# Converting V and the first-MLP weights in smaller pieces, each behind a softmax: an attention-and-MLP kernel on one core

## The chip, the cores and the metric

The kernel runs on one core of one Trainium2 chip. The metric is device time in microseconds (us) of one execution, less is better. Three runs of the kernel before gave 1021.73, 1009.07 and 1010.79 us; their median is 1010.79 us.

## The reference, cut to what matters

Attention over 4 batches, 8 heads, 576 positions and head size 64, with a position bias made by a small network, and then two MLPs over the 2304 tokens of width 512. All arrays are 32 bit floats.

```python
scores = scale * q @ k.T + bias        # bias[h] = relu(x @ w1 + b1) @ w2, x = log1p|i-j| / log1p(max(i,1))
attn = exp(scores - max(scores)); attn = attn / (sum(attn) + 1e-09)
x = attn @ v                           # heads side by side: 2304 x 512
h = max(max(x @ moe_w1, x @ moe_w2), x @ moe_w3)   # 512 -> 768
x = h @ moe_w_out                      # 768 -> 512
h = x @ moe2_w_in                      # 512 -> 2048
g = where(h >= 1, h, where(h <= -1, 0, (h + 1)**2 / 4))
out = g @ moe2_w_out                   # 2048 -> 512
```

In the first MLP `h` is just the largest of the three products. To keep 32 bit accuracy with 16 bit matmuls, an operand is split into a high and a low 16 bit part with a power-of-two scale, and three products of parts are added.

## The kernel before, in words

**Slots.** The queries are cut into five row blocks (four of 128 rows, one of 64). One head of one batch of one row block is a *slot*; there are 144. Slots 0 to 31 are row block 0 (batch b is slots 8b to 8b+7), slots 32 to 63 are row block 1, and so on. The loop at line 903 goes over the slots. For slot i it traces loads ahead (`prefetch`), the score matmuls of the next slot (`emit_s`, L691), the softmax of the slot (`emit_soft`: DVE adds the bias and takes the row extreme, L705; ACT takes the exponent, L707; the probabilities are split into 16 bit parts by ACT L723 and POOL L724 and L725, and a transposing DMA on SP turns them, L727), and the probability-times-V matmuls of slot i-3 (`emit_pv`, L747). In row block 0, odd slots of batches 0 and 1 are turned by TensorE instead (L712 to L719). "The softmax of slot 32" means its L705.

**Work that rides along.** In row block 0 other work is hung on chosen slots:

- `conv_moe(ft)`, one call for each of six columns `ft` of the first MLP's weights (w1, w2, w3). The weights arrive as 64 bit words; `decode` (L462 to L465) makes 32 bit numbers of them, `sum_scale` (L481, L483) finds a scale with TensorE and DVE, and three calls of `split` make the 16 bit parts: ACT writes the high part (L157), DVE the low part (L158), of 128x512 elements each. The slots are in `PRM["cm"]`: 0, 3, 6, 9, 13, 16. Raw weights lie in borrowed places. Column 4's are loaded after column 0's splits, and column 5's (L450) after column 3's splits, into the same bytes. Columns 3 and 5 lie in the buffer of the bias of row block 1.
- V: `v_load(b)` loads batch b (L325, L327), `v_max(b)` finds its scale (L335 and what follows), `v_split(b)` makes two halves (`c` = 0, 1) of 128x1280 elements with the same `split` (L157, L158), clears a strip (POOL, L606) and stores each half to DRAM for the later row blocks (SP, L607, 640 KB each, eight in all). Raw V of batches 1 to 3 shares one place, so the load of batch b+1 waits for the splits of batch b.
- The bias of row block 1: 18 groups (`bias_group`, L389 to L405), traced from slot 16 on and only once all six columns are converted. The softmax of slot 32 needs all 18.

**What sets the order.** The framework gives each instruction a priority by the place where it was traced, simulates the engines with durations of its own, and puts on each engine's queue, of what is ready by that simulation, what was traced first. `sooner("bias")` moves the bias groups 400 places ahead. `tc.issue_after(x)` adds one rule: what is traced inside it and runs on x's engine comes behind x in that engine's queue. `behind(i)` does that with the last L705 for slots below 4. On the chip each queue then runs in that order. `next_mlp` (L784) hands out the first-MLP matmuls (`mlp1`, L802) as long as their column is converted.

Of the kernel before, what the change touches and what calls it, by code (L numbers as in the profile page):

```python
# [20 lines left out]
def kernel(ctx: ExitStack, tc: tile.TileContext, qt, kt, vr, small, mw1, mw2, mw3, mwo, win, wo2, out):  # L21
# [8 lines left out]
    P = 128  # L30
# [15 lines left out]
        vm=[0, 0, 8, 15],  # L46
        vs=[0, 0, 11, 19],
        wo=38,
        cm=[0, 3, 6, 9, 13, 16],
        veng='vv',  # L50
        weng='vvv',
        peng='vv',
# [40 lines left out]
    def st(shape, dt, tag):  # L93
        return sb.tile(shape, dt, tag=tag, name=tag, bufs=BUFS.get(tag, 1))
# [59 lines left out]
    def split(hi, lo, src, scale, eng):  # L154

        if eng == "v":
            A.activation(hi, src, AF.Copy, scale=scale)  # L157
            V.scalar_tensor_tensor(lo, src, scale, hi, ALU.mult, ALU.subtract)  # L158
        else:
            G.tensor_tensor(src, src, (scale.unsqueeze(2) if len(src.shape) == 3 else scale).to_broadcast(src.shape), ALU.mult)  # L160
            A.activation(hi, src, AF.Copy)
            G.tensor_tensor(lo, src, hi, ALU.subtract)

    if True:
# [307 lines left out]
        def by_k(t):  # L472
            return t.rearrange("p (k f) -> p k f", k=KK)
# [12 lines left out]
        def conv_moe(ft):  # L486

            zs, ys = [], []
            for i in range(3):
                ys.append(wm[:, ft, i].rearrange("p s k c -> p (s k c)").bitcast(U32))  # L490
                zs.append(decode(moe_raw[3 * ft + i], None, ys[-1]))
            s = c_sn[:, ft:ft + 1]
            sum_scale(s, ys)
            for i in range(3):
                split(wm[:, ft, i, 0], wm[:, ft, i, 1], by_k(zs[i]), s, WENG[i])
            if ft == 0:
                moe_load(4)
            if ft == 3:
                moe_load(5)

        def conv_wo():

# [90 lines left out]
            wo_done.append(1)  # L593


        def v_split(b):

            if b % 2:
                w = wo.bitcast(F16).rearrange("p f d -> p (f d)")[:, 0:5120].rearrange("p (x s c) -> p x s c", x=2, s=10)
                vv = [w[:, 0], w[:, 1]]  # L600
            else:
                vv = [st([P, 10, 256], F16, "v") for _ in range(2)]
            for c in range(2):
                t = vv[c]
                split(t[:, 0:5], t[:, 5:10], vf(b)[:, :, 256 * c:256 * c + 256], c_sv[:, b:b + 1], VENG[c])
                G.memset(t[64:128, 9], 0.0)  # L606
                SP.dma_start(v_d[b, c], t)  # L607
                kbox[("v", 0, b, c)] = t

        c_s1, c_rb = newcol(), newcol(B)  # L610

# [81 lines left out]
        def halves(t):  # L693
            return t.rearrange("p (a c) -> p a c", a=2)

        last_soft = [None]

        def emit_soft(i):
            u, s = slots[i]
            if s == 0:  # L700
                u.sums = st([P, H], F32, "sums")
            h = s if u.j == SJ else HEADS[s]
            sn = st([P, S], F32, "sp")
            mx = st([P, 1], F32, "mx")
            last_pair[0] = V.tensor_tensor_reduce(halves(sn), sbox.pop(i)[:, :, :288], halves(bias_sb[u.j][:, h]), -0.125, 3e38, ALU.add, ALU.min, mx)  # L705
            pf = sn
            last_soft[0] = A.activation(pf, sn, AF.Exp, scale=-1.0, bias=mx, accum_out=u.sums[:, h:h + 1])  # L707
            if u.j == 0 and u.b < 2 and s % 2:

                pa, pe = mlp_ps(), mlp_ps()[0:64, :P]  # L710
                for c in range(4):
                    T.transpose(pa[:, P * c:P * c + P], pf[:, P * c:P * c + P], ident)  # L712
                T.transpose(pe, pf[:, 512:], ident)
                pt = st([P, 9, P], F16, "pt")
                pa = pa.rearrange("p (c i) -> p c i", c=4)
                A.activation(pt[:, 0:4], pa, AF.Copy)
                A.activation(pt[0:64, 4], pe, AF.Copy)
                V.tensor_tensor(pt[:, 5:9], pa, pt[:, 0:4], ALU.subtract)
                V.tensor_tensor(pt[64:128, 4], pe, pt[0:64, 4], ALU.subtract)  # L719
                ptbox[i] = pt  # L720
                return
            hl = st([P, 2 * S], F16, "phl")
            A.activation(hl[:, :S], pf, AF.Copy)  # L723
            G.tensor_tensor(hl[:, S:S + 64], pf[:, 512:], hl[:, 512:S], ALU.subtract)  # L724
            G.tensor_tensor(hl[:, S + 64:], pf[:, :512], hl[:, :512], ALU.subtract)  # L725
            pt = st([P, 9, P], F16, "pt")
            SP.dma_start_transpose(out=pt, in_=hl)  # L727
            ptbox[i] = pt

        PVSEQ = [(c, c) for c in range(5)] + [(c, 5 + c) for c in range(5)] + [(5 + c, c) for c in range(4)]  # L730
# [53 lines left out]
        def next_mlp(ready):  # L784

            if not mlp_q:
                return None
            if ready:
                return mlp_q.pop(0)
            for x, (f, a) in enumerate(mlp_q):  # L790
                if f is mlp1:
                    return mlp_q.pop(x) if order_of(a[0]) < 2 and a[1] < NF1 - len(conv_left) else None

        def mlp1(key, ft, i, c=slice(0, 256)):

# [94 lines left out]
        for gq in range(0, 18, 2):  # L890
            with tc.issue_after(coef_lo.ins):
                bias_pair(gq)
            while conv_left and PRM["cm"][6 - len(conv_left)] <= gq - 18:
                conv_moe(conv_left.pop(0))
        first_mask.append(last_pair[0])
        emit_s(0)
        with behind(0):
# [20 lines left out]
            return xts[j]  # L918

        early = {}  # L920
        for f, at, *a in [(v_max, "vm", 1), (v_split, "vs", 1), (v_load, "vl", 2), (v_max, "vm", 2), (v_split, "vs", 2), (v_load, "vl", 3), (v_max, "vm", 3), (v_split, "vs", 3)]:
            early.setdefault(PRM[at][a[0]], []).append((f, *a))
        early.setdefault(PRM["vm"][3], []).append((v_scales,))

        def queue_mlp(key, c):
            mlp_q.extend((mlp1, (key, ft, w, c)) for ft in range(NF1) for w in range(3))
# [3 lines left out]
        for i in range(NS + LAG + 1):  # L930
# [20 lines left out]
            if i < NS:  # L951
                with sooner("v"):
                    if PRM["ef"]:
                        for f, *a in early.get(i, ()):
                            with behind(i), tc.issue_after(last_score[0].ins) if f is v_max else nullcontext():
                                f(*a)
                with sooner("w"):
                    while conv_left and PRM["cm"][6 - len(conv_left)] <= i:
                        with behind(i):
                            conv_moe(conv_left.pop(0))  # L960
                b_at, b_n = PRM["bias"][min(u.j, 2)]
                with sooner("bias"):
                    for _ in range(rate("bias", (27 if u.j == 2 else 18) / b_n) if at >= b_at and not conv_left else 0):
                        if bias_q:
                            a = bias_q.pop(0)
                            a = (*a, new_xt(a[0]))
                            if a[0] == SJ:
                                bias_short(*a)
                            else:
                                bias_group(*a, B1[cnt["b"] % len(B1)])  # L970
                                cnt["b"] += 1
# [292 lines left out]
```

## Time and profile before

| | us |
|---|---|
| median of 3 runs (lowest, highest) | 1010.79 (1009.07, 1021.73) |
| profiled execution | 1012.1 |
| its span, first to last instruction | 1010.3 |
| PE busy in the span | 927.0 |
| DVE, ACT, POOL busy in the span | 700.4, 600.4, 511.7 |

Mean granted TensorE clock 0.964 of full speed. Busy time says how much of the span an engine had an instruction in hand, also when that instruction ran at the lower clock. In a row of the trace the square bracket is how long the engine stood idle before the instruction and what released it; "x3" means that three like instructions are merged in one row, and the duration is then that of the three together.

### The profile page before, as it was taken

The numbers are of one execution on the slowest core, as the hardware profiler recorded it, in microseconds if no ns is written. First come the engines' busy times: TensorE is split into PE (matmuls) and PEld (weight loads), VectorE is DVE, ScalarE is ACT, GpSimd is POOL, SyncE is SP. The second block draws the span as 40 slices with busy tenths as digits, with TensorE's granted clock in tenths as the row PEclk, the third lists the DMA queues.
The fourth block names the chain that finished last, engine by engine and source line by source line (L and its number), as shares of the span: only waits on it lengthen the run. The fifth ranks groups of instructions, "written<-read, shape, count | busy, mean of one in ns | idle before, by whom it ended". The sixth has DMA issues, their size and how long they took to land. (4 is left out here: it accounts for less than half of the span.)

```text
span 1010.3 us, 25953 instructions
## 1 busy us (share of the span) xinstructions
PE 927.0 (92%) x10258; PEld 757.4 (75%) x10258; DVE 700.4 (69%) x1551; ACT 600.4 (59%) x1194; POOL 511.7 (51%) x734
## 2 busy tenths in 40 slices
PE   5758889889999999999999888998999999999996
PEld 5636668678888878778777777543588888888885
DVE  8987877767756686556455487886686587586565
ACT  4788865855656545868577689543354444444342
POOL 4132577666777765646457011997134343344442
PEclk8777979999999999999999999999999999999999
DMA  9896989998998979999999654010020010000000
GB/s 301 247 290 140 245 190 229 207 237 170 207 259 186 187 180 209 215 223 235 209 188 197 184 196 137 22 35 8 1 85 22 1 43 23 1 22 13 10 22 22
DMA packets 238970, 141.47 MB, mean 140 GB/s; under 512 B 187520, under 2 KB 217728, under 8 KB 238336
## 3 DMA queue, kind: packets, MB, share of 16 engines
q1 hardware_dynamic: 238688, 139.55, 58.6%
q8 instruction: 80, 1.31, 0.5%
q14 instruction: 42, 0.34, 0.1%
q10 hardware_dynamic: 160, 0.26, 0.1%
HBM read 79.68 MB, written 15.27 MB: 94 GB/s over the span
## 5 line engine op out<-in xcount | busy, mean ns | idle before, releaser
L802 PEld LDWEIGHTS <-aw 128*128 128x128 f16 x2160 | 190.3, 99 | 46.2 <-issue 24.6
L802 PE MATMUL pm<-xT,aw 128*128 128x256 f16 (+1 forms) x1812 | 202.3, 264 | 7.4 <-ACT hl L829 2.6
L725 POOL TENSOR_TENSOR phl<-sp,phl 128x512 f16<-128x512 f32 x136 | 161.3, 1186 | 0.0
L707 ACT ACTIVATE sp<-sp,mx 128x576 f32<-128x576 f32 x144 | 110.4, 767 | 68.0 <-DVE mx L705 67.7
L691 PE MATMUL s<-k,qz 64*128 64x288 f32 (+1 forms) x576 | 126.2, 449 | 15.4 <-DVE mx L705 13.0
L724 POOL TENSOR_TENSOR phl<-sp,phl 128x64 f16<-128x64 f32 x136 | 49.8, 366 | 178.7 <-ACT phl L723 153.2
L705 DVE CUSTOM_DVE_ANT_0 sp<-s,ab 128x576 f32<-128x576 f32 x128 | 93.3, 752 | 28.4 <-POOL phl L725 10.4
L1142 ACT ACTIVATE sp<-pm,vec 128x256 f32<-128x256 f32 x112 | 61.4, 556 | 81.3 <-PE pm L1125 78.2
L691 PEld LDWEIGHTS s<-k,qz 64*128 64x128 f32 (+1 forms) x576 | 69.1, 195 | 34.6 <-DVE mx L705 15.3
L723 ACT ACTIVATE phl<-sp 128x576 f16<-128x576 f32 x136 | 89.8, 672 | 4.7 <-DMA pt<-phl 3.8
L747 PEld LDWEIGHTS <-pt 128*128 128x128 f16 x1792 | 73.0, 100 | 25.2 <-DMA pt<-phl 16.2
L1146 POOL TENSOR_TENSOR hh<-hh 128x128 f32<-128x128 f32 x56 | 32.9, 588 | 106.4 <-DVE hh L1144 90.3
L747 PE MATMUL pav<-v,pt 128*128 128x64 f16 x1568 | 70.5, 196 | 12.3 <-DMA pt<-phl 11.9
L1125 PEld LDWEIGHTS <-ab 128*128 128x128 f16 x756 | 73.8, 98 | 9.2
L1143 DVE SCALAR_TENSOR_TENSOR hh<-pm,vec,sp 128x256 f32<-128x256 f32 x112 | 52.5, 478 | 33.5 <-ACT sp L1142 33.2
L824 PE MATMUL pm<-hh,wo 128*128 128x256 f16 x558 | 71.3, 279 | 2.6 <-POOL hh L814 1.0
L824 PEld LDWEIGHTS <-wo 128*128 128x128 f16 x648 | 62.2, 100 | 14.7 <-issue 6.5
L814 POOL TENSOR_TENSOR hh<-hm,hh 128x256 f16<-128x256 f32 (+1 forms) x60 | 44.8, 746 | 51.9 <-ACT hh L813 51.7
L1164 PEld LDWEIGHTS <-xT 128*128 128x128 f16 x588 | 57.4, 98 | 7.8 <-ACT xT L1151 1.2
L1164 PEld LDWEIGHTS <-wo 128*128 128x128 f16 x588 | 57.5, 98 | 6.7
L809 DVE SCALAR_TENSOR_TENSOR hm<-pm,hm 128x256 f32<-128x256 f32 (+1 forms) x108 | 42.0, 389 | 28.6 <-PE pm L802 12.3
L1147 POOL TENSOR_TENSOR hh<-hh 128x128 f32<-128x128 f32 x56 | 26.2, 468 | 68.6 <-DVE hh L1144 66.3
(300 smaller groups left out, 1999.0 us busy)
## 6 DMA issues: line engine op xcount, KB each, us to landing
k<-in_k_dram SPq DMA_DIRECT2D x64, 288.0 KB, 3.8
v<-v_d SPq DMA_DIRECT2D x24, 640.0 KB, 4.9
ws<-in_moe_w_out_dram SPq DMA_DIRECT2D x15, 512.0 KB, 4.9
ws<-in_moe_w_in_dram SPq DMA_DIRECT2D x9, 512.0 KB, 6.0
x_d<-hl SPq DMA_DIRECT2D x36, 128.0 KB, 2.5
qz<-in_q_dram SPq DMA_DIRECT2D x16, 256.0 KB, 4.5
ab<-in_moe_w_dram SPq DMA_DIRECT2D x8, 512.0 KB, 9.8
qz<-x_d SPq DMA_DIRECT2D x4, 1024.0 KB, 4.8
```

Of the source, the lines that this page charges most:

```text
L691: last_score[0] = T.matmul(sbox[i + r][:, c, :288], q[p, s if u.j == SJ else s // 2], k[p, 288 * c:288 * c + 288], start=True, stop=True)
L705: last_pair[0] = V.tensor_tensor_reduce(halves(sn), sbox.pop(i)[:, :, :288], halves(bias_sb[u.j][:, h]), -0.125, 3e38, ALU.add, ALU.min, mx)
L707: last_soft[0] = A.activation(pf, sn, AF.Exp, scale=-1.0, bias=mx, accum_out=u.sums[:, h:h + 1])
L723: A.activation(hl[:, :S], pf, AF.Copy)
L725: G.tensor_tensor(hl[:, S + 64:], pf[:, :512], hl[:, :512], ALU.subtract)
L747: T.matmul(u.pav[:, 64 * h:64 * h + 64], pt[:, c], v[:, sl, 64 * (h % 4):64 * (h % 4) + 64], **kw)
L802: T.matmul(o, wm[:, ft, i, wp, kk], x_rhs(key, xp, kk) if n == 256 else x_rhs(key, xp, kk)[:, c], start=(x == 0), stop=(x == 11))
L824: T.matmul(pm, wo16[:, ft, wp, P * d:P * d + P], hh[:, ft, hp], start=(ft == 0 and y == 0), stop=(ft == NF1 - 1 and y == 2))
L1125: T.matmul(pm, w[:, wp, kk], x2t[ORDER[y]][:, kk, xp, 256 * sub:256 * sub + 256], start=(x == 0), stop=(x == 11))
L1142: A.activation(r, pm, AF.Relu, scale=c_ch[:, f], bias=c_half)
L1143: V.scalar_tensor_tensor(t, pm, c_c[:, f], r, ALU.mult, ALU.max)
L1164: T.matmul(m[x], gl[:, gp, i], w[:, wp], start=(start and z == 0 and x % 2 == 0), stop=(stop and z == 2 and (x % 2 == 1 or x == 6)))
```

## The change: what it does, and the diff

- `conv_moe` becomes a generator: decode, scale and the first of the three splits come at the column's slot, the second split one slot later, the third one after that. The second and third are traced inside `issue_after` the last L705 and the last L707. The slots of columns 4 and 5 become 12 and 14 (from 13 and 16). The loads that follow columns 0 and 3 come after the third split. The bias groups and `mlp1` ask for finished columns (`conv_done`), where before they asked for started ones.
- `v_split` takes one half at a time, inside the same two `issue_after`. V of batch 1: halves at slots 0 and 8 (both at 0 before). Batch 2: load at slot 8 (2), scale at 12 (8), halves at 13 and 15 (11). Batch 3: load at 15 (11), scale at 19 (15), halves at 20 and 22 (19).
- The stores of V: batch 0 stays with its split; batches 1, 2, 3 are stored at slots 11, 27 and 30, inside `issue_after` the last transposing DMA. Before, each store followed its split.

```diff
-        cm=[0, 3, 6, 9, 13, 16],
+        cm=[0, 3, 6, 9, 12, 14],
...
             for i in range(3):
+                if i:
+                    yield
                 split(wm[:, ft, i, 0], wm[:, ft, i, 1], by_k(zs[i]), s, WENG[i])
             if ft == 0:
                 moe_load(4)
             if ft == 3:
                 moe_load(5)
+            conv_done.append(ft)
+
+        conv_done, conv_open = [], []
...
-        def v_split(b):
+        def v_split(b, cs=(0, 1)):
...
-                vv = [st([P, 10, 256], F16, "v") for _ in range(2)]
-            for c in range(2):
+                vv = {c: st([P, 10, 256], F16, "v") for c in cs}
+            for c in cs:
                 t = vv[c]
                 split(t[:, 0:5], t[:, 5:10], vf(b)[:, :, 256 * c:256 * c + 256], c_sv[:, b:b + 1], VENG[c])
                 G.memset(t[64:128, 9], 0.0)
-                SP.dma_start(v_d[b, c], t)
                 kbox[("v", 0, b, c)] = t
+                if b == 0:
+                    v_store(b, c)
+
+        def v_store(b, *cs):
+
+            for c in cs or (0, 1):
+                SP.dma_start(v_d[b, c], kbox[("v", 0, b, c)])
...
-        last_soft = [None]
+        last_soft, last_turn = [None], [None]
...
-            SP.dma_start_transpose(out=pt, in_=hl)
+            last_turn[0] = SP.dma_start_transpose(out=pt, in_=hl)
...
-                    return mlp_q.pop(x) if order_of(a[0]) < 2 and a[1] < NF1 - len(conv_left) else None
+                    return mlp_q.pop(x) if order_of(a[0]) < 2 and a[1] < len(conv_done) else None
...
-            while conv_left and PRM["cm"][6 - len(conv_left)] <= gq - 18:
-                conv_moe(conv_left.pop(0))
...
-        for f, at, *a in [(v_max, "vm", 1), (v_split, "vs", 1), (v_load, "vl", 2), (v_max, "vm", 2), (v_split, "vs", 2), (v_load, "vl", 3), (v_max, "vm", 3), (v_split, "vs", 3)]:
-            early.setdefault(PRM[at][a[0]], []).append((f, *a))
-        early.setdefault(PRM["vm"][3], []).append((v_scales,))
+        for i, f, *a in [(0, v_max, 1), (0, v_split, 1, (0,)), (8, v_split, 1, (1,)), (8, v_load, 2), (11, v_store, 1), (12, v_max, 2), (13, v_split, 2, (0,)), (15, v_split, 2, (1,)), (15, v_load, 3),
+                         (19, v_max, 3), (19, v_scales), (20, v_split, 3, (0,)), (22, v_split, 3, (1,)), (27, v_store, 2), (30, v_store, 3)]:
+            early.setdefault(i, []).append((f, *a))
...
-                            with behind(i), tc.issue_after(last_score[0].ins) if f is v_max else nullcontext():
-                                f(*a)
+                            with behind(i), tc.issue_after(last_score[0].ins) if f is v_max else tc.issue_after(last_turn[0].ins) if f is v_store else nullcontext():
+                                if f is v_split:
+                                    with tc.issue_after(last_pair[0].ins), tc.issue_after(last_soft[0].ins):
+                                        f(*a)
+                                else:
+                                    f(*a)
                 with sooner("w"):
+                    for g in list(conv_open):
+                        with tc.issue_after(last_pair[0].ins), tc.issue_after(last_soft[0].ins):
+                            if next(g, g) is g:
+                                conv_open.remove(g)
                     while conv_left and PRM["cm"][6 - len(conv_left)] <= i:
                         with behind(i):
-                            conv_moe(conv_left.pop(0))
+                            conv_open.append(conv_moe(conv_left.pop(0)))
+                            next(conv_open[-1])
...
-                    for _ in range(rate("bias", (27 if u.j == 2 else 18) / b_n) if at >= b_at and not conv_left else 0):
+                    for _ in range(rate("bias", (27 if u.j == 2 else 18) / b_n) if at >= b_at and len(conv_done) == NF1 else 0):
```

## Rows read from the trace of the kernel before

**Rows 1.** Windows by stage: us, busy us (count) of each engine, granted clock, DMA share, GB/s.

```profile
31.00:148.00 117.00, 87.95 (x896) 66.53 (x893) 97.24 (x217) 94.80 (x185) 48.36 (x61) 0.80 0.90 216
148.00:175.00 27.00, 24.55 (x549) 23.02 (x547) 22.20 (x44) 13.14 (x35) 22.06 (x27) 1.00 0.95 236
175.00:231.00 56.00, 47.52 (x582) 38.64 (x580) 37.67 (x111) 38.17 (x86) 31.66 (x43) 0.97 1.01 210
231.00:400.00 169.00, 167.10 (x2378) 141.96 (x2376) 117.39 (x279) 100.38 (x244) 117.97 (x155) 1.00 0.94 202
```

**Rows 2.** Timeline of ACT: start us, us, operation; exponents of slots 0 and 31.

```profile
36.79 0.76 ACT L707 ACTIVATE sp<-sp,mx 128x576 f32<-128x576 f32 x1
...
147.89 0.78 ACT L707 ACTIVATE sp<-sp,mx 128x576 f32<-128x576 f32 x1 [0.59 <-DVE mx L705]
```

**Rows 3.** Timeline of DVE and ACT: end of column 5, first bias write, softmax of slot 32.

```profile
134.57 0.79 DVE L158 SCALAR_TENSOR_TENSOR aw<-ab,vec,aw 128x512 f16<-128x512 f32 x1
135.39 0.47 ACT L403 ACTIVATE ab<-pm,vec 128x256 f32<-128x256 f32 x1 [1.26 <-DVE aw L158]
...
174.27 0.76 DVE L705 CUSTOM_DVE_ANT_0 sp<-s,ab 128x576 f32<-128x576 f32 x1 [0.82 <-POOL ab L405]
```

**Rows 4.** Timeline of DVE and PE around 60 us: batch 1's second half, softmax, scores.

```profile
58.10 1.54 DVE L158 SCALAR_TENSOR_TENSOR wo<-ws,vec,wo 128x1280 f16<-128x1280 f32 x1
...
62.56 0.74 DVE L705 CUSTOM_DVE_ANT_0 sp<-s,ab 128x576 f32<-128x576 f32 x1
63.37 2.29 PE L691 MATMUL s<-k,qz 64*128 64x288 f32 x4 [5.41 <-DVE mx L705]
```

**Rows 5.** Timeline of SP, PE and DVE, 61 to 80 us, and one window.

```profile
61.85 1.11 SPq L607 DMA_DIRECT2D v_d<-wo  x1
...
65.82 5.62 SPq L727 DMA_TRANSPOSE pt<-phl  x1
...
77.08 0.93 PE L747 MATMUL pav<-v,pt 128*128 128x64 f16 x14 [3.80 <-DMA pt<-phl]
...
79.54 0.76 DVE L705 CUSTOM_DVE_ANT_0 sp<-s,ab 128x576 f32<-128x576 f32 x1 [4.97 <-PE pm L713]
...
63.00:77.00 14.00, 7.85 (x54) 5.05 (x54) 9.92 (x23) 12.62 (x25) 2.36 (x3) 0.62 1.19 303
```

**Rows 6.** Timeline of ACT, DVE and SP: batch 2's halves, columns 3 and 5.

```profile
94.45 2.60 ACT L157 ACTIVATE v<-ws,vec 128x1280 f16<-128x1280 f32 x2
94.90 0.15 DVE L141 TENSOR_SCALAR vec<-tcol 128x1 uint32<-128x1 uint32 x1
98.77 2.04 ACT L157 ACTIVATE aw<-ab,vec 128x512 f16<-128x512 f32 x3
...
102.09 1.10 SPq L450 DMA_DIRECT2D ab<-in_moe_w_dram  x2
...
111.82 0.68 ACT L462 ACTIVATE ab<-ab 128x512 f32<-128x512 f32 x1 [2.08 <-DMA ab<-in_moe_w_dram]
```

**Rows 7.** Timeline of ACT: batch 3's halves, last decode step of column 5.

```profile
118.85 2.60 ACT L157 ACTIVATE wo<-ws,vec 128x1280 f16<-128x1280 f32 x2
...
122.13 0.65 ACT L465 ACTIVATE aw<-ab 128x512 bf16<-128x512 f32 x1
```

**Rows 8.** Line L158, weight splits on DVE: count, ns min/median/max, first and last start.

```profile
L158 DVE SCALAR_TENSOR_TENSOR aw<-ab,vec,aw x8: 736/766/1402, 61.9 to 134.6; 128x512 f16<-128x512 f32 x8
...
L158 DVE SCALAR_TENSOR_TENSOR aw<-aw,vec x6: 740/746/1683, 66.8 to 86.8; 128x512 f16<-128x512 f32 x6
...
L158 DVE SCALAR_TENSOR_TENSOR aw<-ws,vec,aw x4: 794/1325/1667, 59.6 to 108.2; 128x512 f16<-128x512 f32 x4
```

**Rows 9.** Timeline of SP, 129 to 149 us, and landing times of line L607's stores.

```profile
129.49 17.87 SPq L727 DMA_TRANSPOSE pt<-phl  x6
...
148.49 0.43 SPq L658 DMA_DIRECT2D v<-v_d  x1
...
DMA to landing us min/median/max: 3.3/5.1/9.0
```

## The prediction

> **What bounds the kernel now.** I read the windows by stage first. From 231 to 400 us PE is busy 167.10 of 169 us at full clock: there the kernel is bound by TensorE [rows 1]. Before that it is not. From 31 to 148 us, the 32 slots of row block 0, PE is busy 87.95 of 117 us at a clock of 0.80, DVE 97.24 and ACT 94.80 [rows 1]. So the change works where DVE and ACT set the pace, and a microsecond won there reaches the end only as TensorE idle time, or slow-clock time, that goes away.
>
> I read the timeline next. The exponents of slots 0 and 31 start at 36.79 and 147.89 us [rows 2], so a slot lasts (147.89 - 36.79) / 31 = 3.58 us. Then the softmax stands still until 174.27 us, when POOL has written the last bias group [rows 3]. The reader should see the chain behind it: the first bias write, at 135.39 us, is released by the last DVE split of column 5, which runs from 134.57 to 135.36 us [rows 3]. The 18 groups fill the 39 us between. So what sets slot 32 is when column 5 is finished, not when slot 31 is.
>
> **Ties that are met already.** A tie changes something only where the tied work now runs ahead of the softmax named. Column 3's second and third splits get tied to slots 10 and 11, which at 3.58 us a slot lie near 36.79 + 11 x 3.58 = 76 us; ACT does these splits at 98.77 us [rows 6]. Column 5's get slots 15 and 16 (94 us) and are finished at 135.36 us [rows 3]. Most pieces run five to ten slots behind the slot that traced them, because the scale comes late. The ties bind almost nowhere; what acts is the changed place in the trace and the moved DMAs.
>
> **The parts, one by one.**
>
> *V of batch 1, second half to slot 8.* DVE does it from 58.10 us, ahead of a run of column splits, and PE then waits 5.41 us for the softmax at 62.56 us [rows 4]. One 1.54 us instruction leaves that run. It comes back a few us later on a DVE with 19.8 us idle in 117 [rows 1]. I take 0; the ends are -1.5 and +1.5.
>
> *Stores of batch 1 to slot 11, load of batch 2 behind the second half.* The two stores of 640 KB go out until 61.85 us; a transposing DMA issued at 65.82 us holds SP 5.62 us, PE then stands 3.80 us for such a turned tile at 77.08 us, and DVE 4.97 us at 79.54 us [rows 5]. The DMA share of that stretch is 1.19, the rate 303 GB/s and the clock 0.62 [rows 5]. Two stores are 1.31 MB, at that rate 4.3 us of transfer that is no longer ahead of the turn. I take the whole PE wait, -3.8; the ends are 0 and -5.0. The load itself, some 5 us later, costs nothing: batch 2's scale moves from slot 8 to slot 12, and its halves are done at 94.45 us, 30 us after the old load [rows 6].
>
> *Batch 2's halves from slot 11 to 13 and 15.* Column 3's scale is ready at 94.90 + 0.15 = 95.05 us, but ACT is in the 2.60 us of both V halves and starts the column at 98.77 us [rows 6]. With V traced later, the column, at slots 9 to 11, goes first: -3.7. Against it stands the spreading, which may put the third split two slots back: +7.2. I take -3.7, because the splits are already ready when these slots are long past; both ends stay.
>
> *Stores of batch 2 to slot 27, load of batch 3 to slot 15.* They leave the DMAs free for the raw weights of column 5, issued from 102.09 us, for which ACT waits 2.08 us at 111.82 us [rows 6]. I take -2.1, ends 0 and -2.1.
>
> *Batch 3's halves from slot 19 to 20 and 22.* ACT does both, 2.60 us, right ahead of column 5's last decode step at 122.13 us [rows 7]. One half may step back: -1.3, ends 0 and -2.6. Its DVE part, 2 x 1.54 = 3.1 us, then lies among the bias groups, where DVE is busy 22.20 of 27 us [rows 1]: +3.1, ends 0 and +3.1.
>
> *Columns 4 and 5 from 13 and 16 to 12 and 14.* Column 5 still ends its tracing at slot 16, since its third split comes two slots after 14, and its raw weights are asked for two slots later (11, was 9). I take 0; the ends are -7.2 and +7.2, two slots each way. The six scales, 18 splits and eight halves are the same instructions as before; nothing is added to DVE, ACT or PE.
>
> *Stores of batches 2 and 3 at slots 27 and 30.* They come behind six turns that occupy SP for 17.87 us from 129.49 us, and the load of V for row block 1 at 148.49 us wants batch 2's buffer [rows 9]. New wait: that load, and the k loads and turns behind it on SP, may stand until the store has landed, 3.3 to 9.0 us [rows 9]. The cover is the 26 us in which the softmax waits for the bias anyway [rows 2, 3]; I take 0. Without cover it costs up to 9.0.
>
> *POOL beside the splits.* The 18 weight splits on DVE take 736 to 1683 ns for one shape [rows 8]. By the medians they sum to 8 x 0.766 + 6 x 0.746 + 4 x 1.325 = 15.9 us; all at 0.74 they would take 13.3, all at 1.68 30.2. I take no change, since a burst beside a softmax overlaps POOL as much as single splits do; the ends are -2.6 and +14.3. The Trainium skill (SBUF — State Buffer, section Who interferes with whom) says that a DVE instruction with two SBUF inputs and a GpSimd instruction that reads SBUF exclude each other, the later one waiting for the whole of the earlier one. By that rule single splits, each right behind a softmax whose POOL subtract follows, would tend to the upper end, and the sum below would come out slower than now; the spread of rows 8 agrees that something doubles a split at times, but not that bursts escape it.
>
> **Sum.** At slot 32: -3.8 - 3.7 - 2.1 - 1.3 + 3.1 = -7.8 us. The 3.8 is PE idle time, so it carries to the end. Of the other 4.0 I keep half: PE has only 2.45 us idle from 148 to 175 us, being fed by bias and MLP work, and 8.5 from 175 to 231 [rows 1], so an earlier slot 32 partly moves idle time. That makes -5.8. The profiled execution took 1012.1 us (span 1010.3 and 1.8 around it), 1.3 above the median of 1010.79; so 1006.3 for it and **1005 us** for the median.
>
> **Rivals.**
>
> *A smoother stretch wakes the clock.* PE's 87.95 busy us ran at 0.80, so 17.6 us of them are slow clock, and 29.05 us are idle [rows 1]. If half of the 46.6 goes, the gain is 23 us: 988. For it: the clock is 0.62 right where PE waits for a turned tile [rows 5]. Against it: DVE and ACT are over 80% busy and lose no work. Chance 0.15.
>
> *The change doesn't do what it says.* Since the ties are met already, the bursts stay, and what V gives up around column 3 it takes back among the bias groups: 1011, give or take 4. For it: the lag of five to ten slots. Chance 0.20.
>
> *Column 5 is later.* Its raw weights are asked for after column 3's third split; if the spreading holds for both, that is 7.2 + 7.2 = 14.4 us later than 135.36 us, and the 39 us of bias groups and slot 32 move with it. With the SP wait uncovered, 23.4: 1025 to 1034. It decides from the point where the last split of column 5 ends after 136 us. For it: ACT waits for that load already, so there is no slack. Chance 0.13; beyond 2% in a third of it.
>
> *Splits meet POOL*, as rows 8 allow: -5.8 + 14.3 = +8.5 us, 1019. For it: 1.4 to 1.7 us occur in all three forms; against it: the medians of two forms are the short time. Chance 0.05.
>
> The forecast, 995 to 1010, has 0.47.
>
> **Numbers.** The range 986 to 1021 leaves out part of the clock rival below and most of the column rival above, about 0.2. A difference of 2%, 20 us, is what a measurement of this kernel tells from no change: below 990.6 us lies most of the clock rival and a little of the forecast's end, 0.14; above 1031 a third of the column rival and a little for what the planner reorders elsewhere, 0.06; between, 0.80.
>
> **What would show it.** PE's wait for a turned tile near 77 us is gone and the clock from 63 to 77 us is well above 0.62. Column 3's splits come ahead of batch 2's halves on ACT. The last split of column 5 ends about 128 us and the softmax of slot 32 comes about 167 us. SP shows no long wait at the first V load of row block 1. PE's busy time is about the same or less by its slow clock. I am wrong if column 5 ends later than 136 us, or if slot 32 is earlier and the end is not: then PE's idle time has only moved to 175 to 231 us.

## The result, and the profile after

The changed kernel takes 1015.92 us (median of 20 runs, 1011.71 to 1021.07); 20 runs of the kernel before on the same chip gave 1012.42 us. The ratio is 1.0065, 95% interval [1.0044, 1.0085]: within 2%, but slower, where 5.8 us of gain were forecast. Ratios, clocks and sums over runs are here and below of fast runs alone, without the slowest runs of the kernel before; the medians of all runs above give 1.0035. The profiled execution took 1016.95 us, its span is 1015.2 us (1010.3 before).

The windows by stage of the kernel after, with the stretch of the forecast's turn wait as the last row; columns as in [rows 1]:

```profile
31.00:148.00 117.00, 94.95 (x949) 72.07 (x946) 94.97 (x215) 91.39 (x181) 47.76 (x60) 0.77 0.82 205
148.00:175.00 27.00, 20.19 (x447) 18.95 (x445) 23.35 (x42) 14.08 (x34) 20.20 (x24) 0.94 1.11 280
175.00:231.00 56.00, 49.43 (x603) 39.54 (x601) 37.45 (x107) 39.55 (x91) 35.58 (x48) 0.94 1.01 213
231.00:400.00 169.00, 166.87 (x2386) 141.89 (x2384) 118.64 (x282) 100.70 (x245) 117.85 (x154) 1.00 0.91 199
63.00:77.00 14.00, 7.74 (x75) 4.60 (x72) 12.56 (x28) 12.31 (x25) 5.04 (x7) 0.94 0.92 281
```

Against [rows 1], PE is busy 7 us longer from 31 to 148 us, with 949 matmuls recorded (896) and at a clock of 0.77 (0.80). From 148 to 175 us it is busy 4.4 us less, at a higher DMA share (1.11, was 0.95). In the last row the clock from 63 to 77 us is 0.94, was 0.62 [rows 5], as predicted. But PE is idle there as long as before (6.26 us, was 6.15), over 31 to 77 us as a whole the clock is no higher (before, then after), and in e16, a kernel below with the same queues as after, it is 0.68 from 63 to 77 us:

```profile
31.00:77.00 46.00, 28.69 (x236) 19.82 (x232) 39.94 (x90) 37.66 (x71) 12.31 (x16) 0.79 0.93 259
```

```profile
31.00:77.00 46.00, 33.76 (x253) 23.48 (x250) 39.93 (x90) 35.89 (x67) 13.05 (x16) 0.76 0.78 230
```

```profile
63.00:77.00 14.00, 9.00 (x68) 5.61 (x69) 11.90 (x26) 11.53 (x24) 3.14 (x5) 0.68 0.99 290
```

So most of that rise in the clock belongs to the one execution and not to the change.

Timeline of ACT after, the exponents of slots 0, 31, 32, 52, 100 and 140 (line L718 is L707 of before):

```profile
37.67 0.78 ACT L718 ACTIVATE sp<-sp,mx 128x576 f32<-128x576 f32 x1
...
149.33 0.77 ACT L718 ACTIVATE sp<-sp,mx 128x576 f32<-128x576 f32 x1
...
176.90 0.78 ACT L718 ACTIVATE sp<-sp,mx 128x576 f32<-128x576 f32 x1
...
247.00 0.78 ACT L718 ACTIVATE sp<-sp,mx 128x576 f32<-128x576 f32 x1
...
417.01 0.76 ACT L718 ACTIVATE sp<-sp,mx 128x576 f32<-128x576 f32 x1
...
549.61 0.78 ACT L718 ACTIVATE sp<-sp,mx 128x576 f32<-128x576 f32 x1 [1.12 <-DVE mx L716]
```

The same instants in the kernel before, from slot 32 on:

```profile
175.07 0.78 ACT L707 ACTIVATE sp<-sp,mx 128x576 f32<-128x576 f32 x1 [0.96 <-DVE mx L705]
...
245.05 0.78 ACT L707 ACTIVATE sp<-sp,mx 128x576 f32<-128x576 f32 x1 [0.72 <-DVE mx L705]
...
415.15 0.76 ACT L707 ACTIVATE sp<-sp,mx 128x576 f32<-128x576 f32 x1
...
543.41 0.78 ACT L707 ACTIVATE sp<-sp,mx 128x576 f32<-128x576 f32 x1 [1.12 <-DVE mx L705]
```

Slot 32 is 1.83 us later, slot 52 1.95, slot 100 1.86, slot 140 6.20. So in this pair of profiles nothing is won before slot 32, and over 4 us are lost between slots 100 and 140, where the queues of DVE, ACT, POOL, SP and PE hold the same instructions in the same order in both kernels (they do from slot 52 on). How much of that late loss belongs to the change is taken up with the fourth set.

What the forecast wanted did happen. DVE after: the last split of column 5 (with 134.57 us in [rows 3]). ACT after: column 3's splits and batch 2's halves, in the other order than in [rows 6], and its first bias write:

```profile
126.34 1.44 DVE L158 SCALAR_TENSOR_TENSOR aw<-ab,vec,aw 128x512 f16<-128x512 f32 x1
```

```profile
92.92 2.02 ACT L157 ACTIVATE aw<-ab,vec 128x512 f16<-128x512 f32 x3
105.58 2.61 ACT L157 ACTIVATE v<-ws,vec 128x1280 f16<-128x1280 f32 x2
...
131.04 0.47 ACT L403 ACTIVATE ab<-pm,vec 128x256 f32<-128x256 f32 x1
```

Column 5 ends at 127.8 us instead of 135.4. And still the softmax of slot 32 comes at 176.10 us (174.27): from column 5's end to it there were 39 us, now there are 48. In the second half of that stretch batch 3's halves run, made at 118.85 us before [rows 7]. The timeline of DVE after, and that of PE:

```profile
153.97 3.94 DVE L158 SCALAR_TENSOR_TENSOR wo<-ws,vec,wo 128x1280 f16<-128x1280 f32 x2
```

```profile
152.49 0.31 PE L758 MATMUL pav<-wo,pt 128*128 128x64 f16 x5 [2.28 <-ACT wo L157]
153.90 1.00 PE L393 MATMUL pm<-coef,masks 128*128 128x64 f16 x16 [1.11 <-ACT hm L818]
156.99 1.19 PE L758 MATMUL pav<-wo,pt 128*128 128x64 f16 x30 [0.57 <-POOL wo L611]
```

Three waits, 3.96 us, two of them (2.85 us) for batch 3's halves; the pair of DVE splits takes 3.94 us, not 3.1. My first theory (A) was that these halves among the bias groups give back what column 5 won.

### The profile page after: what moved, and what is told of

Same layout as the page of the kernel before. It is cut to its first block, busy times and chain, and to the rows that moved or that the text cites. A ratio compares the mean times of both kernels' runs of the same rounds, so it can differ in the third digit from the quotient of the medians.

```text
span 1015.2 us, 25950 instructions
## 1 busy us (share of the span) xinstructions
PE 932.2 (92%) x10258; PEld 760.2 (75%) x10258; DVE 701.1 (69%) x1551; ACT 599.3 (59%) x1194; POOL 514.1 (51%) x734
## 5 line engine op out<-in xcount | busy, mean ns | idle before, releaser
L813 PEld LDWEIGHTS <-aw 128*128 128x128 f16 x2160 | 192.5, 100 | 43.1 <-issue 20.8
L813 PE MATMUL pm<-xT,aw 128*128 128x256 f16 (+1 forms) x1812 | 205.1, 266 | 5.0 <-ACT hl L840 3.1
L718 ACT ACTIVATE sp<-sp,mx 128x576 f32<-128x576 f32 x144 | 110.5, 768 | 67.3 <-DVE mx L716 66.7
L835 PE MATMUL pm<-hh,wo 128*128 128x256 f16 x558 | 68.6, 273 | 1.7 <-ACT hh L824 0.9
```

Source lines behind the costliest of these rows:

```text
L813: T.matmul(o, wm[:, ft, i, wp, kk], x_rhs(key, xp, kk) if n == 256 else x_rhs(key, xp, kk)[:, c], start=(x == 0), stop=(x == 11))
L835: T.matmul(pm, wo16[:, ft, wp, P * d:P * d + P], hh[:, ft, hp], start=(ft == 0 and y == 0), stop=(ft == NF1 - 1 and y == 2))
```

## The experiments

Each ratio is to runs of the kernel before on the same chip. The clock is the mean granted TensorE clock over the timed runs; the kernel before had 0.960 to 0.963 in the five sets of its runs. "c5 end" and "slot 32" are the end of column 5's last split and slot 32's exponent in the one profile, us.

| kernel | ratio [95%] | clock | c5 end | slot 32 | slot 52 |
|---|---|---|---|---|---|
| before | 1 | 0.960 to 0.963 | 135.4 | 175.1 | 245.1 |
| after | 1.0065 [1.0044, 1.0085] | 0.952 | 127.8 | 176.9 | 247.0 |
| e1 batch 3 early | 1.0124 [1.0091, 1.0158] | 0.958 | 124.3 | 176.8 | 251.6 |
| e2 stores at split | 1.0075 [1.0046, 1.0104] | 0.955 | 120.8 | 171.8 | 248.4 |
| e3 columns whole | 1.0012 [0.9984, 1.0039] | 0.959 | 128.1 | 173.6 | 243.9 |
| e4 V as before | 1.0094 [1.0066, 1.0123] | 0.952 | 129.6 | 176.2 | 247.6 |
| e5 slots only | 1.0105 [1.0067, 1.0143] | 0.956 | 124.4 | 176.2 | 246.1 |
| e6 steps only | 0.9967 [0.9944, 0.9990] | 0.966 | 129.6 | 170.4 | 232.7 |
| e7 columns late | 1.0066 [1.0042, 1.0090] | 0.951 | 144.5 | 175.1 | 244.8 |
| e8 bias late | 1.0079 [1.0051, 1.0108] | 0.957 | 122.8 | 178.7 | 247.8 |
| e9 old slots | 1.0057 [1.0030, 1.0084] | 0.947 | 124.8 | 175.1 | 244.1 |
| e10 column 5 at 16 | 1.0044 [1.0017, 1.0071] | 0.957 | 129.3 | 182.8 | 248.2 |
| e11 column 4 at 13 | 1.0086 [1.0055, 1.0118] | 0.956 | 128.2 | 175.3 | 251.2 |
| e12 scale tied | 1.0090 [1.0058, 1.0122] | 0.957 | 125.0 | 174.5 | 247.6 |
| e13 steps + batch 3 | 1.0007 [0.9977, 1.0037] | 0.962 | 129.9 | 173.0 | 236.7 |
| e14 steps + batch 2 | 1.0100 [1.0052, 1.0149] | 0.951 | 140.6 | 180.1 | 245.5 |
| e15 steps + stores | 0.9994 [0.9964, 1.0024] | 0.962 | 135.2 | 176.5 | 240.3 |
| e16 queues of after | 1.0040 [1.0010, 1.0070] | 0.954 | 126.4 | 175.9 | 248.8 |
| e17 queues of e6 | 1.0005 [0.9979, 1.0031] | 0.963 | 132.2 | 173.7 | 237.1 |
| e18 batch 2 only | 1.0044 [1.0009, 1.0078] | 0.959 | 144.5 | 176.7 | 249.0 |

Two pairs of kernels have the same queues: after and e16 differ by 0.0025, e6 and e17 by 0.0038. A difference of less than about 0.004 between two of these kernels is therefore not read as one. The instants of a single profile scatter as well: in these two pairs slot 32 differs by 1.0 and 3.3 us, slot 52 by 1.8 and 4.4.

**First set: which part, and is it batch 3?**

e1, in which the products of slots 14 and 15 with V take batch 3's second half instead of batch 1's, because it is made in their buffer so early:

```diff
-(19, v_max, 3), (19, v_scales), (20, v_split, 3, (0,)), (22, v_split, 3, (1,))
+(15, v_max, 3), (15, v_scales), (16, v_split, 3, (0,)), (17, v_split, 3, (1,))
```

> The changed kernel with batch 3's scale at slot 15 and its two halves at 16 and 17 instead of 19, 20 and 22; column 5, the ties and the late stores as changed. Theory A (batch 3's scale and halves stand behind the first bias groups, so that PE waits for them inside the bias chain and the chain gives back the 8 us that column 5 saved): the scale is read at about slot 24 and the halves are made at about slot 26, no PE wait on a V half after 148 us, slot 32's exponent 3 to 8 us before the 176.9 us of the changed kernel (169 to 174), and a ratio to the kernel before of 0.994 to 1.000 where the changed kernel has 1.0065. Theory B (the late stores at slots 27 and 30 meet the turns and loads between 148 and 163 us): nothing changes, slot 32 at 176 to 178 and a ratio of 1.005 to 1.008. Theory C (the loss is made after slot 100, where the order is the same in both kernels): slot 32 may move, the ratio stays between 1.003 and 1.008.

1.0124. The halves are made by 134.8 us, ahead of most bias groups, and the kernel is slower than after. Slot 31 fell back to 164.0 us (149.3), slot 32 stayed at 176.8. But the products of slots 14 and 15 now wait for these halves and run from 130 to 137 us (from 107 to 127 us in after), so e1 by itself doesn't decide on A.

e2:

```diff
-                if b == 0:
-                    v_store(b, c)
+                v_store(b, c)
...
-(11, v_store, 1),
...
-(27, v_store, 2), (30, v_store, 3)
```

> The changed kernel, but each half of V of every batch is stored right where it is made, and not at slots 11, 27 and 30. Theory A: batch 3's halves stay at about slot 32, slot 32's exponent at 175 to 178 us, ratio to the kernel before 1.004 to 1.008. Theory B: the DMA share between 148 and 160 us falls from 1.18 to below 1.0, slot 32's exponent 3 us or more earlier (below 174), ratio 0.997 to 1.002. Theory C: ratio 1.003 to 1.008 whatever slot 32 does.

1.0075: the late stores (B) are not the loss. Slot 32 came 5 us earlier than in after, at 171.8 us, and slot 52 later, at 248.4.

e3:

```diff
-        cm=[0, 3, 6, 9, 12, 14],
+        cm=[0, 3, 6, 9, 13, 16],
...
-                            next(conv_open[-1])
+                            for _ in conv_open.pop(): pass
```

> The changed kernel with the columns of first-MLP weights as before: columns 4 and 5 at slots 13 and 16, the three splits of each called in one go; V as changed. This takes away the gain and leaves the change in V. Theory A: column 5 ends near 134 us again, batch 3's halves still at about slot 32: the slowest of all, slot 32's exponent at 177 to 184 us, ratio to the kernel before 1.007 to 1.014. Theory B: about the same loss as the changed kernel or a little more, 1.005 to 1.010. Theory C: 1.003 to 1.008, with no tie to slot 32.

1.0012, no loss, though batch 3's halves end at 152.7 us there. This refutes A.

e4: `v_split`, its slots, loads and stores as in the kernel before (batch 1 halves at 0; batch 2 load 2, scale 8, halves 11; batch 3 load 11, scale 15, halves 19).

> The changed kernel with everything of V as before (both halves together, stores where they are made, loads, scales and slots as before), and the columns of first-MLP weights as changed. Theory A: column 5 ends near 127 us, batch 3's halves are made at about slot 26, ahead of the bias chain; slot 32's exponent at 167 to 172 us, ratio to the kernel before 0.992 to 0.998: the gain that was forecast. Theory B: the same sign, 0.994 to 1.000, since the stores are early again. Theory C: slot 32 earlier by several us and the ratio nevertheless 1.000 to 1.008.

1.0094. The columns alone are slower than the whole change. All three theories fall or are left without their cause; what e3 and e4 say is that the loss comes with the columns.

**Second set: slots or steps?** e5 is the kernel before with `cm=[0, 3, 6, 9, 12, 14]`. e6 is the kernel before with the generator, the ties and `conv_done`, at 13 and 16. e7 is e3 with `cm=[0, 3, 6, 9, 15, 19]`. e8 is the changed kernel with `bias=[[20, 10], [12, 16], [3, 26]]`, where 20 was 12.

> The kernel before with only the slots of columns 4 and 5 changed, from 13 and 16 to 12 and 14. Nothing of V, no steps, no ties. Theory D (moving columns 4 and 5 ahead does the harm: column 5 and the first bias groups come ahead of the softmaxes of slots 24 to 31, which starve TensorE, and TensorE then runs longer at its low clock): ratio to the kernel before 1.005 to 1.010, mean granted clock 0.950 to 0.956 where the kernel before has about 0.960, last split of column 5 before 130 us, and slot 32 nevertheless within 3 us of 175. Theory E (the steps do the harm, because the matmuls of the first MLP and the bias groups now wait until a column's third split is traced): ratio 0.998 to 1.002, clock 0.958 to 0.963. Theory A (batch 3's halves too late): the halves are made at slot 27, ahead of most bias groups, so 0.994 to 1.000.

> The kernel before with the three splits of a column in steps at separate slots, with the two ties and with finished instead of started columns asked for; columns 4 and 5 at 13 and 16 and V as before. Theory D: ratio to the kernel before 0.998 to 1.003, clock 0.957 to 0.963, last split of column 5 at 130 to 137 us. Theory E: ratio 1.005 to 1.010, clock 0.950 to 0.956.

> The kernel of the third experiment (V as changed, columns in one go) with columns 4 and 5 at slots 15 and 19: the other direction. Column 5's splits and all bias groups then stand behind the softmax of slot 31. Theory D, if it goes both ways: slots 24 to 31 come 5 us or more earlier than in the kernel before, clock 0.960 or higher, ratio 0.992 to 1.000. If only the sum of the work before slot 32 counts: slot 32 at 172 to 178 us and a ratio of 0.998 to 1.003. If column 5 is after all what slot 32 follows, as the forecast had it: column 5 ends after 145 us, slot 32 at 180 us or later, ratio 1.005 to 1.015.

> The changed kernel with the bias groups of row block 1 traced from slot 20 on instead of slot 16; columns 4 and 5 early, as changed. Theory D, if the harm is in the early bias groups: the softmaxes of slots 26 to 31 come 3 us or more earlier than in the changed kernel, clock 0.957 to 0.962, ratio to the kernel before 0.998 to 1.003. If the harm is in the early columns themselves: as the changed kernel, 1.004 to 1.009, clock 0.950 to 0.955.

e5 1.0105, e6 0.9967: two slot numbers cost 10 us, the steps cost nothing. e7 is slower as well, so the old slots lie between two worse ones. e8 stays with after: it is not the early bias groups. In e5 the mechanism seemed to stand in two rows, ACT and PE:

```profile
111.28 0.67 ACT L462 ACTIVATE ab<-ab 128x512 f32<-128x512 f32 x1 [4.63 <-DMA ab<-in_moe_w_dram]
```

```profile
115.70 0.27 PE L481 MATMUL pm<-aw,ones 128*128 128x128 bf16 x1 [3.42 <-ACT aw L465]
```

Column 5 is asked for earlier, but its raw weights still come only behind column 3's splits; so ACT waits 4.63 us (2.08 in [rows 6]) and PE 3.42 us, at the scale matmul of column 5. The kernel after has the same PE wait, at 110.47 us, and so has each of e1, e2, e4 and e8 (2.8 to 4.2 us); before, e3, e6 and e7 have none. In after it is not the raw weights that ACT is late for: batch 2's halves (105.58 us, above) stand between its decode steps of column 5.

```profile
110.47 0.59 PE L481 MATMUL pm<-aw,ones 128*128 128x128 bf16 x4 [2.83 <-ACT aw L465]
```

**Third set: is it this wait (theory W)?** e9 and e10 are the changed kernel with `cm` ending in 13, 16 and in 12, 16; e11 in 13, 14. e12 keeps 12, 14 and moves the scale matmuls behind a later score matmul:

```diff
+            if ft == 5:
+                yield
+            with tc.issue_after(last_score[0].ins) if ft == 5 else nullcontext():
-            sum_scale(s, ys)
+                sum_scale(s, ys)
```

> The changed kernel with one thing undone: columns 4 and 5 at slots 13 and 16 as in the kernel before. Steps, ties and everything of V as changed. Theory W (the loss comes from one wait: with columns 4 and 5 at 12 and 14 the scale matmuls of column 5, L481, stand so early on TensorE's queue that TensorE waits 2.8 to 4.2 us for ACT's decode of that column near 110 us, and a long stretch at the low clock follows): no wait of TensorE over 1 us at L481, granted clock 0.960 or higher, last split of column 5 at 125 to 135 us, ratio to the kernel before 0.993 to 1.000. Theory V (the late stores and the late halves of V cost something of their own, hidden so far): ratio 1.002 to 1.008.

> The changed kernel with column 4 at slot 12 as changed and column 5 at slot 16 as before. Theory W: the scale matmuls of column 5 stand behind more scores on TensorE's queue, no wait over 1 us at L481, clock 0.960 or higher, ratio 0.994 to 1.001. If it is column 4's slot that does the harm: ratio 1.004 to 1.010, clock 0.950 to 0.956.

> The changed kernel with column 5 at slot 14 as changed and column 4 at slot 13 as before. Theory W: TensorE waits 2 us or more at L481 for the decode of column 5, a low-clock stretch of 10 us or more follows, clock 0.950 to 0.957, ratio 1.004 to 1.010. If it is column 4's slot that does the harm: ratio 0.994 to 1.001.

> The changed kernel with its slots 12 and 14, but the scale matmuls and splits of column 5 are traced one slot after its decode, and the scale matmuls come behind the last score matmul traced by then on TensorE's queue. This aims at the wait itself. Theory W: the wait at L481 is 1.5 us or less, the low-clock stretch behind it is gone or under 8 us, clock 0.957 or higher, ratio 0.995 to 1.003. If the early place of column 5 among the softmaxes does the harm, and not that wait: ratio 1.004 to 1.009 although the wait is shorter.

PE at column 5's scale in e12:

```profile
108.51 0.60 PE L481 MATMUL pm<-aw,ones 128*128 128x128 bf16 x4
113.50 0.61 PE L481 MATMUL pm<-aw,ones 128*128 128x128 bf16 x4
115.60 0.63 PE L481 MATMUL pm<-aw,ones 128*128 128x128 bf16 x4
```

The wait is gone, the 1.0090 is not; and e9 and e10, without the wait as well, are at 1.0057 and 1.0044. W is refuted as the cause. e11 (wait of 3.65 us) is at 1.0086. And e13 of the next set has the longest wait of all at this place and no loss (1.0007):

```profile
116.95 0.58 PE L481 MATMUL pm<-aw,ones 128*128 128x128 bf16 x4 [4.31 <-ACT aw L465]
```

And e9 shows that the parts don't add: steps alone (e6) and V with whole columns (e3) cost nothing, together they do.

**Fourth set: which part of V, on top of e6?**

```diff
e13  (15, v_load, 3), (19, v_max, 3), (19, v_scales), (20, v_split, 3, (0,)), (22, v_split, 3, (1,))
e14  (8, v_load, 2), (12, v_max, 2), (13, v_split, 2, (0,)), (15, v_split, 2, (1,)), (15, v_load, 3)
e15  (11, v_store, 1), (27, v_store, 2), (30, v_store, 3)
```

> The kernel with steps alone (ratio 0.9967 to the kernel before), and of V only batch 3 as changed: its load at slot 15, scale at 19, halves at 20 and 22. The halves then stand behind column 5 and the first bias groups. Theory A2 (batch 3's halves among the bias groups take the gain back): ratio 1.003 to 1.009, clock 0.955 or lower, slot 32's exponent 4 us or more behind that of steps alone (170.5 us). Else 0.995 to 1.000.

> The kernel with steps alone, and of V only batch 2 as changed: load at slot 8, scale at 12, halves at 13 and 15; column 3 then goes ahead of batch 2's halves, the step for which the forecast had -3.7 us. If that term holds: ratio 0.991 to 0.996. Theory A2: no loss of its own, 0.994 to 1.000, unless batch 3's halves are pushed back with it. If moving batch 2 is what takes the gain back: 1.003 to 1.009.

> The kernel with steps alone, and of V only the stores as changed: batch 1 at slot 11, batch 2 at 27, batch 3 at 30, each behind the last turn. The forecast's term for the early stores is -3.8 us: ratio 0.991 to 0.996. Theory B: the late stores meet the turns near 150 us, 1.002 to 1.008. If stores don't matter: 0.995 to 0.999.

> The changed kernel without the two ties on the second and third splits of the columns, and with first-MLP matmuls that ask for started columns again. Every engine's queue is the same to the last instruction. All theories: the time of the changed kernel, ratio to the kernel before 1.004 to 1.009, clock 0.949 to 0.956. As a second profile of these queues: if the loss is made before slot 52, its exponent of slot 52 is 2 us or more behind the 245.1 us of the kernel before, and slots 100 to 140 take within 1 us of the 128.3 us of the kernel before; if it is made in that late stretch, slots 100 to 140 take 131 us or more again (132.6 in the first profile).

e14 alone is slow: 1.0100, against 0.9967 and (e17, below) 1.0005 for the two kernels from which it differs in batch 2 and the load behind it only. Windows by stage, e6 and then e14:

```profile
31.00:148.00 117.00, 90.03 (x1059) 69.64 (x1056) 100.65 (x231) 98.68 (x197) 50.87 (x64) 0.87 0.96 236
148.00:175.00 27.00, 22.86 (x465) 21.24 (x463) 20.22 (x49) 13.44 (x35) 21.72 (x28) 1.00 0.82 185
```

```profile
31.00:148.00 117.00, 90.58 (x881) 68.80 (x877) 92.60 (x214) 96.13 (x187) 44.11 (x62) 0.74 0.93 232
148.00:175.00 27.00, 24.35 (x499) 22.57 (x498) 19.45 (x39) 9.75 (x28) 18.24 (x22) 0.88 0.55 169
```

PE is busy the same 90 us, but 881 matmuls are recorded in it instead of 1059, at a clock of 0.74 instead of 0.87 (0.82 in e17, with the queues of e6). e13 and e15 show no loss that this measurement can tell. e16 has 1.0040, in line with after within the scatter, so the ties on the columns and the finished-column condition of `mlp1` do nothing: the queues are the same without them. Its exponents of slots 100 and 140:

```profile
419.29 0.77 ACT L718 ACTIVATE sp<-sp,mx 128x576 f32<-128x576 f32 x1
...
553.43 0.78 ACT L718 ACTIVATE sp<-sp,mx 128x576 f32<-128x576 f32 x1 [1.12 <-DVE mx L716]
```

134.1 us, after 132.6, before 128.3: the late loss is there in both profiles of these queues. The waits of PE in that stretch (us in total, times, longest), before (415 to 545 us), after (417 to 550) and e16 (419 to 554), one fence each:

```profile
PE pav L747 <- DMA pt<-phl: 1.1, 1, 1.1
PE pav L743 <- DMA pt<-phl: 0.3, 1, 0.3
```

```profile
PE pav L758 <- DMA pt<-phl: 3.4, 4, 1.3
PE pav L754 <- DMA pt<-phl: 1.0, 1, 1.0
```

```profile
PE pav L758 <- DMA pt<-phl: 2.6, 3, 1.2
PE pav L754 <- DMA pt<-phl: 1.4, 1, 1.4
```

4.4 and 4.0 us for turned tiles instead of 1.4, in queues that are the same: the transfers fall differently. The other traces don't bear this stretch out as the place of the loss. From slot 100 on the queues are the same in all 20 kernels, and slots 100 to 140 take 127.5 us in e5 (1.0105) and 133.0 us in e15 (0.9994). Over the 20 profiles that time has no relation to the ratio (a correlation of -0.2) and hardly any to the waits for turned tiles (0.2). The instant of slot 100 does go with the ratio (0.8), that of slot 32 less (0.4). So what the kernels differ in lies mostly ahead of slot 100 and not all of it ahead of slot 32, and theory C is not borne out.

**Fifth set.** e17 is e6 without the ties and with started columns; e18 is the kernel before with e14's line for batch 2.

> The kernel with steps alone, less the two ties on the columns and with first-MLP matmuls that ask for started columns: what is left of the change is that the second and third split of a column are traced one and two slots later, and the bias groups after them. Every engine's queue is that of the kernel with steps alone. If its gain is real: ratio to the kernel before 0.994 to 0.999, clock 0.963 to 0.968, slot 52's exponent 232 to 240 us (245.1 in the kernel before). If it was scatter: 0.999 to 1.003.

> The kernel before with one change: batch 2 is loaded at slot 8, its scale found at 12 and its halves made at 13 and 15. Column 3 then goes ahead of batch 2's halves on ACT; batch 3's halves and column 5 stand at the softmax of slot 29 on ACT's queue instead of 24 and 27. If the forecast's term holds: ratio 0.995 to 0.998. If moving batch 2 costs by itself: ratio 1.004 to 1.013, clock 0.950 to 0.957, column 5's last split after 136 us, the fifth and following bias groups later. If it costs only together with the steps: 0.998 to 1.002.

e17 has 1.0005: the gain of e6 is not confirmed, although slot 52 is 8 us early again (237.1 us); 5 of the 8 are left at slot 100 and 1.5 at slot 140. e18 has 1.0044, just above the scatter: moving batch 2 costs by itself, though its clock, 0.959, is above what was expected for that. No kernel here is shown to beat the kernel before.

## Why the prediction was wrong, point by point

**The step that failed: "what sets slot 32 is when column 5 is finished, not when slot 31 is."** Column 5 was finished 7.6 us earlier, as forecast, and slot 32 came 1.8 us later. Over the 20 profiles of the table column 5 ends anywhere from 120.8 to 144.5 us, and slot 32 comes from 170.4 to 182.8 with hardly any relation (a correlation of 0.2): the 39 us behind it that the forecast moved along as a block are 31 us long in e7 and 56 in e8; the earliest column (e2) has 51 left, the latest (e7, e18) 31 and 32, and e7's slot 32 is at 175.1 us, exactly where it was before. The row that I read as the releaser of the chain ([rows 3]: the first bias write waits for column 5's last split) only says which instruction came last in that order. By the code, the softmaxes, splits and bias groups to be done before slot 32 are the same in each kernel, so that finishing one of them earlier may only put it ahead of the others. Where the bias groups begin late, the softmaxes of slots 24 to 31 pass them (e7: first bias write at 144.6 us, slot 31 at 134.8; e4: 131.8 and 153.9), but only loosely so: the correlation over the 20 profiles is -0.4. So what slot 32 follows in place of column 5 is argued from the code and not shown.

**"Column 3 first": -3.7 us, the wrong sign.** Column 3 did go ahead of batch 2's halves, by 12.7 us on ACT. Moving batch 2, with batch 3's load behind it, gives 1.0044 by itself on the kernel before (e18), +4 us, and on steps alone 1.0100 (e14), 0.0095 to 0.0133 or 10 to 13 us more than these. Column 5 then ends 9 and 8 to 11 us later (144.5 and 140.6 us), the sign that the forecast had set for its rival "Column 5 is later"; slot 32 moves with it by 1.6 us in e18 and by 6 to 10 in e14. The bound of +7.2 was set for another cause, a third split put two slots back.

**Slots of columns 4 and 5: 0 us, ends of 7.2 either way.** On the kernel before they cost 1.0105 (e5), 10.6 us, beyond the end. That column 5's raw weights would not come earlier was in the text; that ACT and PE would then stand waiting for them at the head of their queues (e5) was not priced. The waits don't account for the loss, which stays without a shown cause.

**Stores of batch 1: -3.8.** The wait for a turned tile near 77 us is gone and the clock from 63 to 77 us is up, as predicted, but neither is shown to come from the stores: e2, e6 and e17 store batch 1 at its split and have no such wait either, e15 moves the stores and has one of 1.07 us, and the clock was largely luck (0.94 in after, 0.68 in e16). The term took the whole wait as a gain; PE is idle as long in that stretch as before, now for DVE (among it 2.82 us for a softmax, at 74.67 us). At the end no gain shows: stores alone (e15) give 0.9994 on top of kernels with 0.9967 and 1.0005.

**Stores of batch 2 late, load of batch 3 late: -2.1.** ACT no longer waits for column 5's raw weights, as predicted; its first decode step after has no idle time before it ([rows 6]: 2.08 us). What it was worth at the end no run shows.

```profile
102.77 0.67 ACT L462 ACTIVATE ab<-ab 128x512 f32<-128x512 f32 x1
```

**Batch 3 among the bias groups: +3.1.** They do lie there, with 3.94 us on DVE; the 2.85 us in which PE waits for the halves were not in the text. Its price alone (e13, 1.0007) is within the scatter.

**Late stores at SP, 0, and POOL beside the splits, 0.** No price of the late stores shows at the end: e2 recovers nothing. The 18 column splits keep DVE busy for 15.3 us after and 17.8 before (the forecast's 15.9 was a sum of medians), 2.5 us less, near the lower end of -2.6 and not 0. The Trainium skill (SBUF — State Buffer, section Who interferes with whom) has a rule by which the forecast saw single splits tend to the upper end; they don't here. Batch 3's two DVE splits take 2.0 us each, against 1.54 before, and no run shows what slowed them.

**"The change doesn't do what it says"** was right for the ties on the columns (e16) and wrong in the conclusion, 1011: the places in the trace did act.

**"A smoother stretch wakes the clock"** named a quantity that did move, but the other way. By the clock the ends of the table fall into two groups: all ten kernels at 1.0065 and above, after among them, have 0.951 to 0.958, all five at 1.0012 and below have 0.959 to 0.966. The four between, at 1.0040 to 1.0057, don't fall into line: e9, at 1.0057, has the lowest clock of all, 0.947, and e18, at 1.0044, has 0.959. Within one kernel, over 296 runs, a run that loses 1 us more to the low clock (span times one minus the clock) takes 0.45 us longer. After loses 48.5 us that way, the kernel before 37.1 to 40.0 in its five sets: at 0.45 that is 3.8 to 5.1 us, of the order of the loss. This is an association; no experiment set the clock by itself, so whether it causes the loss or only follows TensorE's waits stays open. Open, too, is why the parts don't add (e3, e6, e9).

## What to carry to other kernels

A releaser in the chain of waits names the last of several works that share the engines; before a gain on it is carried to the end, ask what else must be done by that point, and whether finishing this work earlier only puts it ahead of the rest. A conversion asked for earlier than its data can come turns into a wait at the head of an in-order queue, and it holds what is queued behind it (ACT 4.63 us, then PE 3.42 us in e5); but a wait found in the trace is not yet the cause of the loss, as e12 and e13 show. Where a planner reorders everything behind a small edit, time each part alone, and repeat one kernel, before believing a difference of a few tenths of a per cent.

## What was not expected of the hardware

Kernels whose queues are the same instruction for instruction differ from one set of runs to the next by 0.0025 and 0.0038 in the ratio. The same queues between slots 100 and 140 take 127.5 to 134.1 us over the 20 profiles; PE's idle time there, 7.6 to 12.8 us, goes with it (a correlation of 0.8), its waits for turned tiles hardly (0.2). And the granted clock of the stretch from 31 to 148 us is 0.74 in e14 and 0.87 in e6 for the same 90 us of busy TensorE: its busy time alone says little of the work done.
